# Block means turned in quarters of the TensorE array, the last result tile written in halves, and a new instruction order

## Chip, cores and metric

The kernel runs on one core of a Trainium2 chip. The metric is the device time of one execution in microseconds (us); the median of the runs shown is compared before and after.

## Reference

Sparse attention followed by a two-layer feed-forward part. q, k and v are 4 batch elements x 8 heads x 768 positions x 64. Every query attends to the keys less than 16 positions away, and to 24 block keys, each the maximum over 32 positions; the block values are the means over the same 32 positions.

```
k_sum = k.reshape(B, H, nb, 32, D).max(axis=3)
v_sum = v.reshape(B, H, nb, 32, D).mean(axis=3)
scores_l = where(|i - j| < 16, scale * q @ k.T, -1e9)
scores_s = scale * q @ k_sum.T + log(32)
a = softmax(concat(scores_l, scores_s))
x = a @ concat(v, v_sum)             # then to 3072 tokens x 512
h = x @ w_in                         # 512 x 2048
out = (h - tanh(h)) @ w_out          # 2048 x 512
```

## The kernel before

**Units of work.** The 3072 tokens are cut into 8 units u of 384 tokens, two for each batch element b = u // 2. Attention goes by head pairs p (4 in a unit), each as a chain: turn q and k on TensorE ("turn"), scores into PSUM banks pS0 and pS1, minimum, exponential, sum and normalisation, turning the probabilities ("p turn"), and the product with the values into bank pX ("values"). The 24 block keys and block values lie beside the window's keys and values in the tiles k and vw. The feed-forward part goes by 16 blocks f of the hidden size: products into bank pH ("in"), tanh and its relatives on ScalarE, one product on GpSimd or VectorE ("g"), a split into a high and a low part (gh, gl), and products into the three result banks pY0 to pY2 ("out"). From u = 2 on, units are taken in pairs and the first products come from sums of weights that lie in DRAM (scr) and are loaded into wraw.

**Block means.** For b = 0 and 1, `place_v` makes the mean of four heads (a group g) with 24 matmuls whose four outputs lie at PSUM partitions 0, 32, 64 and 96, each a quarter of the array's columns, and copies them head by head into the tile `mean`, on ScalarE or VectorE. For b = 2 and 3, `sum_chunks` adds the 32 positions of each block on GpSimd (vacc) and takes their maximum on VectorE (kacc). Then `finish_k` turns kacc in bank pS1 and copies it to th, and `finish_v` brings vacc into `mean`: four matmuls with slices of the identity (the "mean turn"), all into partitions 0 to 23 of pS1 at columns 64 x head, and one ScalarE copy of 24x256 with the factor 1/32 ("mean out"). That happens four times in the kernel: two groups for b = 2, two for b = 3. `put_mean` then sends `mean` to vw by DMA from SyncE ("mean put", vw<-mean).

**Results.** `store_y` copies each result tile of 128x512 from its pY bank by ScalarE and stores it by one DMA of 256 KB ("y out", "y store"). The last unit's three tiles end the kernel. After that the program reads one number, the largest sum of squares that it saw ("seen"), and leaves out a second, exact version of itself if it is small.

**Order.** No engine's order is written by hand. Each operation is given to `Plan.add` with an assumed cost on each engine that may do it, its reads and its writes. `Plan.schedule` then lists all operations once: at each step the engine that comes free first takes the ready operation with the highest level. A level is the longest path of assumed costs to the end, plus a number from the table BIAS for that single operation and a number from KB for its kind and phase. SL holds, by kind, phase and engine, how much sooner a second engine must be for it to get the operation. The order of all engines, SyncE's DMA queue among them, and the choice of engine thus come from these tables. The instructions of nearly all operations are recorded under line 76, the one that passes them on, so the profile is read by tiles.

Of the kernel before, what the change touches and what calls it, by code (L numbers as in the profile page):

```python
# [47 lines left out]
SIGNED = set()

SL = {('g', 0, 'vector'): 2, ('g', 1, 'vector'): 0, ('g', 2, 'vector'): -0.3, ('g high', 0, 'vector'): 2.5, ('g high', 1, 'vector'): -0.6, ('g high', 2, 'vector'): 0.3, ('g low', 0, 'vector'): 4, ('g low', 1, 'vector'): -0.6, ('g low', 2, 'vector'): 0, ('k first', 0, 'vector'): 0.3, ('k first', 1, 'vector'): 1.5, ('k first', 2, 'vector'): -0.6, ('k high', 0, 'vector'): 4, ('k high', 1, 'vector'): 2, ('k high', 2, 'vector'): -0.3, ('k keep', 0, 'vector'): 2.5, ('k keep', 1, 'vector'): 2, ('k keep', 2, 'vector'): 1, ('k move', 0, 'vector'): -0.6, ('k move', 0, 'gpsimd'): 1, ('k move', 1, 'vector'): -0.3, ('k move', 1, 'gpsimd'): 4, ('k move', 2, 'vector'): 4, ('k move', 2, 'gpsimd'): 2, ('mean out', 0, 'vector'): 0.6, ('mean out', 1, 'vector'): 4, ('mean out', 2, 'vector'): 2, ('normal', 0, 'scalar'): 2, ('normal', 0, 'gpsimd'): 2.5, ('normal', 1, 'scalar'): 0.6, ('normal', 1, 'gpsimd'): -0.3, ('normal', 2, 'scalar'): 0, ('normal', 2, 'gpsimd'): 0, ('p out', 0, 'vector'): 4, ('p out', 1, 'vector'): 4, ('p out', 2, 'vector'): 0, ('part', 0, 'vector'): 0.3, ('part', 1, 'vector'): 0, ('part', 2, 'vector'): 0.6, ('q high', 0, 'vector'): 1.5, ('q high', 1, 'vector'): 1, ('q high', 2, 'vector'): 0.6, ('s high', 0, 'vector'): -0.3, ('s high', 1, 'vector'): 4, ('s high', 2, 'vector'): -0.3, ('s low', 0, 'gpsimd'): 2, ('s low', 1, 'gpsimd'): 2, ('s low', 2, 'gpsimd'): 0.6, ('s mix', 0, 'gpsimd'): -0.6, ('s mix', 1, 'gpsimd'): 0.3, ('s mix', 2, 'gpsimd'): 4, ('s whole', 0, 'gpsimd'): 1.5, ('s whole', 1, 'gpsimd'): 1, ('s whole', 2, 'gpsimd'): 0, ('sum guard', 0, 'gpsimd'): 0.3, ('sum guard', 1, 'gpsimd'): 1.5, ('sum guard', 2, 'gpsimd'): -0.3, ('top high', 0, 'scalar'): -0.6, ('top high', 1, 'scalar'): -0.3, ('top put', 0, 'vector'): 0, ('top put', 0, 'scalar'): 1, ('top put', 1, 'vector'): 2.5, ('top put', 1, 'scalar'): 0.6, ('top put', 2, 'vector'): 2.5, ('top put', 2, 'scalar'): 0.3, ('w high part 2', 0, 'vector'): 0.3, ('w high part 2', 1, 'vector'): 2.5, ('w high part 2', 2, 'vector'): 2.5, ('w scale', 0, 'vector'): -0.6, ('w scale', 1, 'vector'): 0.3, ('w scale', 2, 'vector'): 0, ('x high', 0, 'vector'): 0.6, ('x high', 1, 'vector'): 4, ('x high', 2, 'vector'): 2.5, ('x low', 0, 'gpsimd'): -0.3, ('x low', 1, 'gpsimd'): 0, ('x low', 2, 'gpsimd'): 2, ('x mix', 0, 'gpsimd'): 0.3, ('x mix', 1, 'gpsimd'): 0, ('x mix', 2, 'gpsimd'): 1.5, ('x whole', 0, 'vector'): 0.6, ('x whole', 1, 'vector'): -0.3, ('x whole', 2, 'vector'): 2}  # L50

KB = {('chunk load', 0): 434.7, ('chunk max', 0): 88.2, ('chunk max', 1): -2.7, ('chunk sum', 0): -220.5, ('chunk sum', 1): -359.7, ('const', 0): -85, ('const', 1): -136.2, ('const', 2): -292.2, ('exp', 0): -33.6, ('g', 0): 13.2, ('g high', 0): -241.1, ('g low', 0): -310.4, ('in first', 0): -71.1, ('in first', 1): -182.2, ('inverse', 0): 28.8, ('join', 0): -293.9, ('join', 1): -75.7, ('k first', 0): -518.8, ('k first', 1): 106.5, ('k first', 2): 448.9, ('k high', 0): -153.3, ('k high', 1): -35.8, ('k keep', 0): 101, ('k keep', 1): -596.6, ('k keep', 2): -249.5, ('k load', 1): -310.2, ('k load', 2): -1.6, ('k move', 0): 111.7, ('k move', 1): -80.4, ('k move', 2): -200.1, ('key turn', 0): -255.8, ('key turn', 1): 120.7, ('key turn', 2): -1.5, ('mean out', 0): -253.8, ('mean out', 1): -79.7, ('mean put', 0): 93.1, ('mean put', 1): -73.6, ('mean put', 2): -2.8, ('mean turn', 1): 1.3, ('mean turn', 2): 20.1, ('min', 0): -0.6, ('normal', 0): 1.9, ('out first', 0): -357.5, ('out first', 1): -259.5, ('p out', 0): -27.4, ('p turn', 0): -1, ('part', 0): 89.2, ('part', 1): 385.1, ('q high', 0): -508.8, ('q load', 0): -35.5, ('q load', 1): 1.5, ('s high', 0): -41.2, ('s high', 1): 1.8, ('s high', 2): -462.5, ('s load', 0): -243.6, ('s load', 1): 1.6, ('s low', 0): 24.9, ('s low', 2): 102.6, ('s mix', 0): -358.8, ('s mix', 2): -480, ('s store', 0): -187, ('s store', 1): 0.7, ('s store', 2): -123.9, ('s whole', 0): 102.7, ('s whole', 1): -1.9, ('s whole', 2): 130.5, ('scores', 0): 1.4, ('seen', 0): 90.1, ('seen', 1): -77, ('seen', 2): -428.9, ('seen max', 0): -210.6, ('seen max', 1): 358.7, ('seen max', 2): 451.2, ('seen turn', 0): -0.7, ('seen turn', 1): 422.3, ('seen turn', 2): -9.1, ('series', 0): -201.9, ('square', 0): -65.5, ('sum', 0): 2.4, ('sum', 1): 419.6, ('sum', 2): -916.3, ('sum guard', 0): 59.1, ('tanh', 0): -2.1, ('top high', 0): 522.9, ('top high', 1): -162.7, ('top max', 0): 10.2, ('top max', 1): 238.5, ('top max', 2): -133.8, ('top pre', 0): -43.1, ('top pre', 1): 183.6, ('top pre', 2): -330.8, ('top put', 0): 0.1, ('top put', 1): -866.6, ('top put', 2): -26.1, ('top turn', 1): -172.1, ('top turn', 2): -472.6, ('turn', 0): 50.1, ('turn', 1): 211.7, ('v load', 1): -28.3, ('values', 1): -139.4, ('w high part 2', 0): -476.2, ('w high part 2', 1): 18.5, ('w high part 2', 2): -45.7, ('w load', 2): 227.6, ('w low', 2): 254.3, ('w low part 2', 0): -652.5, ('w low part 2', 1): -319, ('w low part 2', 2): -478.7, ('w scale', 2): -271.5, ('w shift', 1): 10.3, ('w shift', 2): -314.7, ('w sign', 0): -86.7, ('w sign', 2): -126.7, ('x high', 0): 646, ('x high', 1): -12, ('x low', 0): 282.9, ('x low', 2): -2, ('x mix', 0): 644.6, ('x mix', 1): 18, ('x whole', 0): -1.1, ('x whole', 1): -240.3, ('y out', 0): 157.1, ('y store', 0): -402.7}

HALF = {'const': (12, 12), 'k load': (33, 52), 'q load': (12, 24), 'top pre': (16, 16), 'v load': (44, 82), 'top turn': (8, 8), 'top max': (8, 8), 'q turn': (6, 15), 'q high': (12, 30), 'k turn': (6, 15), 'k high': (6, 15), 'top put': (7, 15), 'scores': (6, 14), 'sum': (8, 8), 'min': (30, 84), 'exp': (30, 84), 'sum out': (8, 8), 'sum guard': (5, 26), 'inverse': (5, 26), 'normal': (30, 84), 'p turn': (15, 42), 'p out': (15, 41), 'mean turn': (2, 4), 'mean out': (2, 4), 'mean put': (6, 14), 'values': (4, 4), 'x whole': (4, 9), 'w load': (13, 32), 'w scale': (12, 32), 'w shift': (12, 32), 'w low': (11, 32), 'w sign': (11, 32), 'w high part 2': (11, 32), 'w low part 2': (7, 32), 'in': (5, 33), 'square': (5, 33), 'tanh': (5, 32), 'series': (5, 32), 'g': (4, 32), 's store': (5, 48), 'out': (7, 96), 'x high': (0, 10), 'x low': (0, 10), 'y out': (0, 6), 'y store': (0, 6), 'g high': (0, 16), 'g low': (0, 16), 's whole': (0, 16), 's mix': (0, 32), 's high': (0, 16), 's low': (0, 16), 'chunk load': (0, 10), 'chunk max': (0, 4), 'chunk sum': (0, 4), 's load': (0, 3), 'x mix': (0, 1), 'top high': (0, 0), 'part': (0, 0), 'join': (0, 0), 'seen': (0, 0), 'seen turn': (0, 0), 'seen max': (0, 0), 'w high part': (3, 26), 'w low part': (3, 26), 'w sign 1': (4, 12), 'w sign 2': (4, 12), 'top low': (1, 2), 'cube': (2, 18), 'big': (2, 17), 'direct': (2, 17), 'pick': (2, 17), 'q low': (0, 2), 'q again': (0, 2), 'k low': (0, 2), 'k again': (0, 2)}


# [254 lines left out]
def program(  # L311
# [433 lines left out]
    def finish_v(b, g, tag):  # L745
        acc, ps = ("acc", 1, b, g), bank(("mv", b, g), tag)

        def go():
# [668 lines left out]
```

## Time and profile before

| what | value |
|---|---|
| median of 3 runs | 685.15 us (684.44, 685.15, 686.1) |
| the profiled execution, its own time | 684.28 us |
| its span, first to last instruction | 682.6 us |
| granted TensorE clock, mean | 0.996 |
| TensorE busy | 659.1 us, 97% |
| ScalarE, VectorE, GpSimd busy | 491.2, 417.4, 206.8 us |
| HBM traffic over the span | 172 GB/s |

PE is TensorE's matmul, PEld its weight load, DVE VectorE, ACT ScalarE, POOL GpSimd, SPq SyncE's queue, which issues the DMAs. A row of the timeline has the start, the time, the engine, the line, the operation, the tiles written and read, and in brackets the idle time before it with what ended it. A matmul's time runs until its results are out, so that rows of PE overlap; the distance between starts is what a matmul takes of the array. In a table of stages, the busy time of each engine stands with its count of instructions, then the granted clock (PEclk), the share of the DMA engines and the bytes moved.

### The profile page before, as it was taken

The page shows a single profiled execution, that of the slowest core. Times are in us where ns is not written, and L with a number is a line of the kernel's source. Part 1 is how long each engine was busy: PE and PEld are TensorE (multiplying, and loading weights), DVE is VectorE, ACT ScalarE, POOL GpSimd, SP SyncE. Part 2 cuts the span into 40 slices and gives each one's busy share as a digit, 9 for nine tenths or more (in the row PEclk, how much of TensorE's full clock was granted, in tenths as well). Part 3 has the DMA queues.
Part 4 walks back from the last instruction along what each step waited for, and adds up shares of the span by engine and source line. Part 5 has one row for each costly group of instructions (what it writes and reads, how often), then busy time and mean ns, then how long its engine had stood idle before and what let it go on. Part 6 is the DMA issues. An engine that isn't in the chain of part 4 may idle for free.

```text
span 682.6 us, 14370 instructions
## 1 busy us (share of the span) xinstructions
PE 659.1 (97%) x4885; PEld 549.1 (80%) x4885; DVE 417.4 (61%) x1183; ACT 491.2 (72%) x1445; POOL 206.8 (30%) x336
## 2 busy tenths in 40 slices
PE   7899999899999989999999999999999999999995
PEld 6665555478888877999888889899889889999884
DVE  3889988868897476555584574445576443323551
ACT  4888576778787787768984786766679946555882
POOL 2012222325355545312375642321124110000230
PEclk9999999999999998999999999999999999999999
DMA  8899999853766864785576456758435214453101
GB/s 242 218 260 286 292 291 271 275 156 136 214 190 192 269 186 135 192 220 172 133 233 187 119 139 211 221 156 213 141 116 158 105 62 147 161 170 123 48 1 52
DMA packets 145151, 121.05 MB, mean 177 GB/s; under 512 B 85036, under 2 KB 110892, under 8 KB 145068
## 3 DMA queue, kind: packets, MB, share of 16 engines
q1 hardware_dynamic: 145068, 120.03, 59.6%
q8 instruction: 41, 0.67, 0.4%
q14 instruction: 42, 0.34, 0.2%
HBM read 94.57 MB, written 23.07 MB: 172 GB/s over the span
## 4 chain that ended last, share of the span: by engine, by line
PE 85%; DMA 7%; DVE 3%; ACT 1%; SPq 1%; issue 1%; POOL 1%; ACTq 0%; POOLq 0%; DVEq 0%
PE pY L76 37%; PE pH L76 36%; PE pS L76 7%; PE pX L76 5%; DMA tmp<-in_k_dram 2%; SPq L76 1%; DMA wraw<-in_moe_w_in_dram 1%; DMA gu<-in_v_dram 1%; DMA wh<-in_k_dram 1%; DVE kacc L76 1%; DVE wraw L76 1%; DMA vw<-mean 1%; DMA rawk<-in_k_dram 1%; DMA out_dram<-tmp 1%; DMA scr<-wraw 1%
## 5 line engine op out<-in xcount | busy, mean ns | idle before, releaser
L76 PE MATMUL pY<-wf,gh 128*128 128x512 f32 x432 | 178.1, 439 | 2.9 <-POOL gh L76 2.9
L76 PE MATMUL pH<-wh,wraw 128*128 128x384 f32 x672 | 175.5, 342 | 0.1
L76 PE MATMUL pY<-wh,gh 128*128 128x512 f32 x336 | 137.0, 408 | 0.0
L76 PE MATMUL pY<-wh,gl 128*128 128x512 f32 x336 | 132.7, 395 | 0.0
L76 PEld LDWEIGHTS pH<-wh,wraw 128*128 128x128 f32 x672 | 121.4, 189 | 8.8 <-issue 1.2
L76 PE MATMUL pH<-wf,wraw 128*128 128x384 f32 x309 | 104.2, 337 | 0.0
L76 ACT ACTIVATE prob<-prob,stat 128x118 f32<-128x118 f32 x247 | 92.5, 384 | 12.7 <-DVE stat L76 11.3
L76 PEld LDWEIGHTS pY<-wf,gh 128*128 128x128 f32 x432 | 80.2, 189 | 25.4 <-issue 10.6
L76 PEld LDWEIGHTS pY<-wh,gl 128*128 128x128 f32 x336 | 63.2, 188 | 13.8
L76 POOL TENSOR_TENSOR gu<-gu,gt 128x384 f32<-128x384 f32 x31 | 33.7, 1087 | 128.8 <-ACT gu L76 127.7
L76 PEld LDWEIGHTS pY<-wh,gh 128*128 128x128 f32 x336 | 63.3, 188 | 10.9 <-issue 1.7
L76 ACT ACTIVATE gu<-gu 128x384 f32<-128x384 f32 x128 | 66.6, 521 | 1.8
L76 PE MATMUL pH<-o,wf 128*128 128x384 f32 x188 | 65.1, 442 | 2.0 <-ACT o L76 1.7
L76 PEld LDWEIGHTS pH<-wf,wraw 128*128 128x128 f32 x309 | 58.1, 188 | 0.0
L76 ACT ACTIVATE gu<-pH 128x384 f32<-128x384 f32 x65 | 31.7, 488 | 36.5 <-PE pH L76 33.5
L76 DVE CUSTOM_DVE_ANT_0 prob<-pS,mask 128x118 f32<-128x118 f32 x180 | 40.1, 275 | 28.8 <-PE pS L76 28.8
L76 PEld LDWEIGHTS pH<-o,wf 128*128 128x128 f32 x188 | 34.8, 189 | 19.7 <-issue 2.9
L76 ACT ACTIVATE gv<-pH 128x384 f32<-128x384 f32 x60 | 29.0, 484 | 27.0 <-PE pH L76 26.8
L76 DVE TENSOR_TENSOR gl<-gu,gh 128x384 fp32r<-128x384 f32 x43 | 27.0, 628 | 32.6 <-ACT gh L76 31.8
L76 POOL COPY k<-th 64x72 f32<-64x72 f32 (+1 forms) x45 | 12.7, 282 | 107.9 <-PE pS L76 86.3
L76 DVE TENSOR_TENSOR gu<-gu,gt 128x384 f32<-128x384 f32 x39 | 23.3, 596 | 35.9 <-ACT gu L76 35.8
L76 POOL TENSOR_TENSOR gl<-gu,gh 128x384 fp32r<-128x384 f32 x27 | 29.2, 1081 | 50.8 <-ACT gh L76 28.9
(211 smaller groups left out, 1242.5 us busy)
## 6 DMA issues: line engine op xcount, KB each, us to landing
wraw<-scr SPq DMA_DIRECT2D x75, 512.0 KB
wraw<-in_moe_w_in_dram SPq DMA_DIRECT2D x16, 512.0 KB
wraw<-in_moe_w_out_dram SPq DMA_DIRECT2D x16, 512.0 KB
scr<-wraw SPq DMA_DIRECT2D x16, 512.0 KB
rawq<-in_q_dram SPq DMA_DIRECT2D x42, 128.0 KB
out_dram<-tmp SPq DMA_DIRECT2D x21, 256.0 KB
wraw<-scr SPq DMA_DIRECT2D x21, 256.0 KB
scr<-wh SPq DMA_DIRECT2D x16, 256.0 KB
```

Of the source, the lines that this page charges most:

```text
L76: return lambda *args, **kwargs: self._tc.keep_in_program_order(op(*args, **kwargs))
```

## The change

1. In `finish_v` the four matmuls write at partitions 32 x head, columns 0 to 63, in place of partitions 0 to 23, columns 64 x head. The copy into `mean` is four copies of 24x64, each on ScalarE or VectorE. The assumed costs follow: 0.2 for the turn in place of 0.56, and 0.2 or 0.17 for each copy in place of one of 0.28.
2. In `store_y` the last tile of the last unit is copied in two halves of 128x256, the first by ScalarE and the second by VectorE, and stored by two DMAs of 128 KB (1024-byte rows in place of 2048).
3. The tables BIAS, SL and KB are new. Of 3304 entries of BIAS 11 stay as they are and 3349 are there after; of the 83 entries of SL 17 stay; of KB none.

```
-                tensor.matmul(at(ps)[:NB, D * hh:D * (hh + 1)], ident[:96, NB * hh:NB * (hh + 1)], at(acc)[:96], start=True, stop=True)
-        do("mean turn", PE, 0.56, go, r=[(acc, 0), IDENT], w=[(ps, 0)])
-        do("mean out", ACT, 0.28, lambda: scalar.activation(mean[32 * g:32 * g + NB], at(ps)[:NB, :HG * D], AF.Copy, scale=1.0 / 32), r=[(ps, 0)], w=MEANS[g])
+                tensor.matmul(at(ps)[32 * hh:32 * hh + NB, :D], ident[:96, NB * hh:NB * (hh + 1)], at(acc)[:96], start=True, stop=True)
+        do("mean turn", PE, 0.2, go, r=[(acc, 0), IDENT], w=[(ps, 0)])
+        for n in range(HG):
+            either("mean out", {ACT: 0.2, DVE: 0.17}, lambda e, n=n: copy(e, mean[32 * g:32 * g + NB, D * n:D * (n + 1)], at(ps)[32 * n:32 * n + NB, :D], 1.0 / 32), r=[(ps, 0)], w=[MEANS[g][n]])
...
-        do("y out", ACT, 0.48, lambda: scalar.activation(at(ys), at(y), AF.Copy, scale=1.0 / (3.0 * EA * EC) if small_only else 1.0), r=[(y, 0)], w=[(ys, 0)])
-        r = u * U + P * i
-        dma("y store", lambda: sync.dma_start(out[r:r + P, :], at(ys)), P * DM * 4, 2048, r=[(ys, 0)])
+        r, by, n = u * U + P * i, 1.0 / (3.0 * EA * EC) if small_only else 1.0, 2 if end and i == NT - 1 else 1
+        for h in range(n):
+            x = slice(DM // n * h, DM // n * (h + 1))
+            if h:
+                do("y out", DVE, 0.335, lambda x=x: vector.tensor_scalar(at(ys)[:, x], at(y)[:, x], by, None, op0=ALU.mult), r=[(y, 0)], w=[(ys, h)])
+            else:
+                do("y out", ACT, 0.48 / n, lambda x=x: scalar.activation(at(ys)[:, x], at(y)[:, x], AF.Copy, scale=by), r=[(y, 0)], w=[(ys, h)])
+            if n > 1:
+                dma("y store", lambda x=x: sync.dma_start(out[r:r + P, x], at(ys)[:, x]), P * DM * 4 // n, 1024, r=[(ys, h)])
+        if n == 1:
+            dma("y store", lambda: sync.dma_start(out[r:r + P, :], at(ys)), P * DM * 4, 2048, r=[(ys, 0)])
```

More of the change, by code (lines that the diff above doesn't have):

```diff
@@ new lines @@
+SL = {('g', 0, 'vector'): 0, ('g', 1, 'vector'): 0.3, ('g', 2, 'vector'): 0.3, ('g high', 0, 'vector'): 2, ('g high', 1, 'vector'): 0.3, ('g high', 2, 'vector'): 0.3, ('g low', 0, 'vector'): -0.6, ('g low', 1, 'vector'): 0.3, ('g low', 2, 'vector'): 0, ('k first', 0, 'vector'): 1, ('k first', 1, 'vector'): 0, ('k first', 2, 'vector'): -0.3, ('k high', 0, 'vector'): 2.5, ('k high', 1, 'vector'): 2, ('k high', 2, 'vector'): 0, ('k keep', 0, 'vector'): 2.5, ('k keep', 1, 'vector'): 1, ('k keep', 2, 'vector'): 2.5, ('k move', 0, 'vector'): 0.3, ('k move', 0, 'gpsimd'): 2, ('k move', 1, 'vector'): 0, ('k move', 1, 'gpsimd'): 1.5, ('k move', 2, 'vector'): 2.5, ('k move', 2, 'gpsimd'): 1.5, ('mean out', 0, 'vector'): 2, ('mean out', 1, 'vector'): 1.5, ('mean out', 2, 'vector'): -0.6, ('normal', 0, 'scalar'): 2, ('normal', 0, 'gpsimd'): 2.5, ('normal', 1, 'scalar'): 0.6, ('normal', 1, 'gpsimd'): -0.6, ('normal', 2, 'scalar'): -0.3, ('normal', 2, 'gpsimd'): -0.6, ('p out', 0, 'vector'): 4, ('p out', 1, 'vector'): 2, ('p out', 2, 'vector'): 0, ('part', 0, 'vector'): 0, ('part', 1, 'vector'): 1, ('part', 2, 'vector'): 0.3, ('q high', 0, 'vector'): 1.5, ('q high', 1, 'vector'): 0.3, ('q high', 2, 'vector'): 4, ('s high', 0, 'vector'): 1.5, ('s high', 1, 'vector'): 4, ('s high', 2, 'vector'): 2, ('s low', 0, 'gpsimd'): 0.3, ('s low', 1, 'gpsimd'): 1.5, ('s low', 2, 'gpsimd'): 0, ('s mix', 0, 'gpsimd'): 0.3, ('s mix', 1, 'gpsimd'): 2, ('s mix', 2, 'gpsimd'): 4, ('s whole', 0, 'gpsimd'): 2.5, ('s whole', 1, 'gpsimd'): 2, ('s whole', 2, 'gpsimd'): 0.6, ('sum guard', 0, 'gpsimd'): -0.3, ('sum guard', 1, 'gpsimd'): 1.5, ('sum guard', 2, 'gpsimd'): -0.6, ('top high', 0, 'scalar'): -0.6, ('top high', 1, 'scalar'): -0.3, ('top put', 0, 'vector'): 0.6, ('top put', 0, 'scalar'): 2.5, ('top put', 1, 'vector'): 4, ('top put', 1, 'scalar'): 4, ('top put', 2, 'vector'): 1, ('top put', 2, 'scalar'): 2, ('w high part 2', 0, 'vector'): 0.6, ('w high part 2', 1, 'vector'): 4, ('w high part 2', 2, 'vector'): 0.6, ('w scale', 0, 'vector'): 0.6, ('w scale', 1, 'vector'): -0.6, ('w scale', 2, 'vector'): -0.3, ('x high', 0, 'vector'): 1, ('x high', 1, 'vector'): 2.5, ('x high', 2, 'vector'): 1.5, ('x low', 0, 'gpsimd'): 0.3, ('x low', 1, 'gpsimd'): 0.6, ('x low', 2, 'gpsimd'): 1.5, ('x mix', 0, 'gpsimd'): 2, ('x mix', 1, 'gpsimd'): 2, ('x mix', 2, 'gpsimd'): 1.5, ('x whole', 0, 'vector'): 2, ('x whole', 1, 'vector'): -0.3, ('x whole', 2, 'vector'): 1}
@@ new lines @@
+KB = {('chunk load', 0): -89.6, ('chunk max', 0): -366.8, ('chunk max', 1): 28.1, ('chunk sum', 0): 57.1, ('chunk sum', 1): 190.1, ('const', 0): 65.2, ('const', 1): 43.2, ('const', 2): -106.1, ('exp', 0): 243.7, ('g', 0): -0.4, ('g high', 0): 224, ('g low', 0): 581.2, ('in first', 0): -297, ('in first', 1): -122.7, ('in first', 2): 3.9, ('inverse', 0): 159.2, ('join', 0): 267.6, ('join', 1): 205.6, ('k first', 0): 207.9, ('k first', 1): -179.9, ('k first', 2): 120.7, ('k high', 1): -5, ('k keep', 0): -62.1, ('k keep', 1): -284.8, ('k keep', 2): 236.2, ('k load', 0): 0.8, ('k load', 1): -360, ('k move', 0): 211.7, ('k move', 1): 31.1, ('k move', 2): -140, ('key turn', 0): -515.5, ('key turn', 1): 651.5, ('key turn', 2): -247, ('mean out', 0): -207.7, ('mean out', 1): 254.1, ('mean put', 0): 31.1, ('mean put', 1): -1.9, ('mean turn', 2): -184.3, ('min', 0): 2, ('normal', 0): -184.1, ('out first', 0): -160.8, ('out first', 1): -350.3, ('p out', 0): -85.4, ('p turn', 0): 73.1, ('part', 0): 447.8, ('part', 1): 235.8, ('q high', 0): -17.3, ('q high', 2): -171.7, ('q load', 0): 48.1, ('q load', 2): -1.1, ('s high', 0): 422.3, ('s high', 2): -195.5, ('s load', 0): 39.6, ('s low', 0): -326.9, ('s low', 2): -95.2, ('s mix', 0): -30.5, ('s mix', 2): 31.9, ('s store', 0): -226.5, ('s store', 2): 42.5, ('s whole', 0): -65.9, ('s whole', 1): -4.1, ('s whole', 2): 175.3, ('scores', 0): 63.7, ('seen', 0): 104.1, ('seen', 1): 81.7, ('seen', 2): -463.2, ('seen max', 0): 101.2, ('seen max', 1): 138.7, ('seen max', 2): -333.8, ('seen turn', 0): 12.5, ('seen turn', 1): -347, ('seen turn', 2): -55.1, ('series', 0): 69.8, ('square', 0): -2.3, ('sum', 0): -14, ('sum', 1): 22.3, ('sum', 2): 149.9, ('sum guard', 0): 88.2, ('tanh', 0): -77.3, ('top high', 0): -474, ('top high', 1): 245.5, ('top max', 0): -240.8, ('top max', 1): -368.4, ('top max', 2): -125, ('top pre', 0): -10, ('top pre', 1): 165.1, ('top pre', 2): 306.5, ('top put', 0): -149.7, ('top put', 1): -548, ('top put', 2): -247.2, ('top turn', 1): 299.5, ('top turn', 2): -288.3, ('turn', 0): -175.4, ('turn', 1): -6.8, ('v load', 0): 25.6, ('values', 0): 20.7, ('values', 1): -90.2, ('w high part 2', 0): -63.2, ('w high part 2', 1): -228.7, ('w high part 2', 2): -172.1, ('w load', 0): -70.7, ('w load', 1): -15.4, ('w load', 2): -449.1, ('w low', 0): -229.2, ('w low', 1): 8.3, ('w low', 2): 154, ('w low part 2', 0): 54.4, ('w low part 2', 1): -9, ('w low part 2', 2): -241.3, ('w scale', 0): -180.3, ('w scale', 1): 3, ('w scale', 2): 70.5, ('w shift', 0): 173.9, ('w shift', 1): 4.6, ('w shift', 2): 120.4, ('w sign', 0): 37.6, ('w sign', 2): -204.1, ('x high', 0): 80.1, ('x high', 1): -57, ('x low', 0): 329.4, ('x low', 1): -4.3, ('x mix', 0): 230.5, ('x mix', 1): -410.1, ('x whole', 0): 60.1, ('x whole', 1): -34.8, ('y out', 0): -294.9, ('y store', 0): 23.1}
```

4 lines of the change are left out of this document (1 added, 3 removed).

## Prediction

> **What bounds the kernel now.** I read the page's busy line and chain first, then a table of three stages, then two of its rows more finely, and last PE's own waits.
>
> ```profile
> span 682.6 us, 14370 instructions
> PE 659.1 (97%) x4885; PEld 549.1 (80%) x4885; DVE 417.4 (61%) x1183; ACT 491.2 (72%) x1445; POOL 206.8 (30%) x336
> PE 85%; DMA 7%; DVE 3%; ACT 1%; SPq 1%; issue 1%; POOL 1%; ACTq 0%; POOLq 0%; DVEq 0%
> ```
> ```profile
> 0.00:40.00 40.00, 31.80 (x572) 26.48 (x572) 25.02 (x112) 25.13 (x86) 6.94 (x34) 1.00 0.86 243
> 40.00:640.00 600.00, 591.59 (x4160) 493.47 (x4157) 376.35 (x1041) 439.30 (x1292) 190.51 (x294) 1.00 0.62 183
> 640.00:682.60 42.60, 35.66 (x159) 29.11 (x157) 16.04 (x32) 26.73 (x68) 9.30 (x8) 0.98 0.11 40
> ```
> ```profile
> 120.00:160.00 40.00, 37.08 (x290) 26.63 (x288) 31.73 (x92) 30.18 (x96) 14.81 (x15) 1.00 0.68 207
> 240.00:280.00 40.00, 36.61 (x308) 31.80 (x310) 24.81 (x68) 30.57 (x97) 19.25 (x38) 0.96 0.59 160
> ```
> ```profile
> PE pS L76 <- POOL ident L76: 4.3, 1, 4.3
> PE pY L76 <- POOL gh L76: 2.9, 1, 2.9
> PE pX L76 <- DMA rawk<-in_k_dram: 2.1, 1, 2.1
> ```
>
> TensorE is the bound: busy 97% of the span, 85% of the chain. Its idle time lies in three places. The start has 40.00 - 31.80 = 8.2 us, of which 4.3 is the wait for the identity that GpSimd makes first; no part of the change touches that. The 600 us between have 600 - 591.59 = 8.41 us, and two of the fifteen 40 us stages in them hold 2.92 + 3.39 = 6.31 of it. The end has 42.60 - 35.66 = 6.94 us. So work taken from PE anywhere in the middle counts almost fully, and what an order can win there is mostly those two stages. They are two accidents:
>
> ```profile
> 127.84 5.08 POOL L76 TENSOR_TENSOR gh<-gu,gt 128x384 f32<-128x384 f32 x1 [4.68 <-DVE tmp L76]
> 132.97 1.13 PE L76 MATMUL pY<-wf,gh 128*128 128x512 f32 x2 [2.92 <-POOL gh L76]
> ```
> ```profile
> 256.71 0.44 PE L76 MATMUL pX<-ident,rawk 128*128 128x128 f32 x2 [2.09 <-DMA rawk<-in_k_dram]
> ```
> ```profile
> 256.70:258.00 1.30, 1.29 (x8) 1.09 (x8) 1.30 (x3) 1.22 (x4) 1.14 (x3) 0.86 1.05 386
> 258.00:259.50 1.50, 1.50 (x6) 1.21 (x5) 1.05 (x3) 1.13 (x5) 1.34 (x3) 0.50 1.00 292
> 259.50:261.00 1.50, 1.50 (x6) 1.50 (x5) 0.00 (x0) 0.61 (x2) 1.02 (x4) 0.50 0.68 205
> 261.00:264.00 3.00, 3.00 (x17) 2.71 (x17) 1.47 (x3) 1.78 (x5) 2.60 (x6) 0.99 0.36 88
> ```
>
> At 127.84 one GpSimd product took 5.08 us, and PE waited 2.92 for it. At 256.71 PE waited 2.09 us for a load of keys, and straight after it ran for 3.00 us at a granted clock of 0.50 and for 1.30 us at 0.86: 3.00 x 0.50 + 1.30 x 0.14 = 1.7 us more, 3.8 in all. The Trainium skill ("TensorE: Matmul & The Clock Gate", Part 1) says that the clock halves only after about one idle window of 3.4 us, in windows that run free of the kernel. This trace differs: 2.09 us were enough here, and 2.92 us at 132.97 were not. By the page alone the second accident would cost 2.1 us.
>
> **The mean turn (part 1).** Before:
>
> ```profile
> 234.48 0.34 PE L76 MATMUL pH<-wf,wraw 128*128 128x384 f32 x1
> 234.75 0.63 PE L76 MATMUL pS<-vacc,ident 96*24 96x64 f32 x8
> 235.31 0.50 PE L76 MATMUL pY<-wh,gh 128*128 128x512 f32 x1
> ```
> ```profile
> L76 PE MATMUL pS<-vacc,ident x32: 216/219/237, 234.8 to 396.3; 96*24 96x64 f32 x32
> ```
> ```profile
> 93.52 0.88 PE L76 MATMUL pS<-wh,wh 128*32 128x64 f32 x48
> 94.33 0.70 PE L76 MATMUL pY<-wf,gh 128*128 128x512 f32 x1
> ```
>
> One turn (four matmuls, eight records) holds the array 235.31 - 234.75 = 0.56 us. The quarter form has a row already: `place_v`'s 48 records, also in quarters, hold it 94.33 - 93.52 = 0.81 us, so a round of eight takes 0.81 / 6 = 0.135. A lone round cannot overlap the next one. It lies between 0.135 and the 0.219 of one record; I take 0.20, nearer the latter. That saves 0.56 - 0.20 = 0.36 a turn, 4 x 0.36 = **-1.44 us**. All four lie in the middle, where PE is the bound. If a turn is followed by a wait for a load, its 0.36 only lengthens that wait, so the gain could shrink towards 0. The lower end is 4 x (0.56 - 0.135) = -1.7. The upper end is that the array must empty once more on each side of the quarter form; the nearest row for that is the gap that PE's weight queue shows before the old form:
>
> ```profile
> 234.75 0.46 PEld L76 LDWEIGHTS pS<-vacc,ident 96*24 96x24 f32 x8 [0.25 <-issue]
> ```
>
> A turn would then take 0.20 + 2 x 0.25 = 0.70 in place of 0.56, and the four +0.6. I keep -1.44, because the old form already enters through a gap and `place_v`'s 0.81 us is taken to the next product's start, its way out included. The Trainium skill ("TensorEngine Tiling (Array Packing)", Key Properties) says that changing the tiling mode drains TensorE, which speaks against the change; no run here separates that drain from the gap above, and by the page alone the turn would gain less than 1.44.
>
> **Mean out.** One copy becomes four:
>
> ```profile
> L76 ACT ACTIVATE mean<-pS 24x64 f32<-24x64 f32 x8 | 1.7, 216 | 0.1
> L76 ACT ACTIVATE mean<-pS 24x256 f32<-24x256 f32 x4 | 1.5, 371 | 0.9 <-PE pS L76 0.8
> L76 DVE COPY mean<-pY 24x64 f32<-24x64 f32 x2 | 0.4, 214 | 0.3 <-PE pY L76 0.3
> ```
> ```profile
> 267.22 0.61 PE L76 MATMUL pS<-vacc,ident 96*24 96x64 f32 x8 [0.43 <-ACT th L76]
> 267.87 0.37 ACT L76 ACTIVATE mean<-pS 24x256 f32<-24x256 f32 x1 [0.79 <-PE pS L76]
> 268.61 0.33 PE L76 MATMUL pS<-k,q 64*64 64x118 f32 x4
> ```
>
> That is 4 x 0.216 - 0.371 = 0.49 us more ACT or DVE time at each turn, 2.0 in all. ACT is idle for 28% of the span and DVE for 39%, which hides it. The cover fails only where the next scores want bank pS1 soon. That is the turn at 267.22: copy until 268.24, scores at 268.61. Afterwards the turn ends 0.36 earlier, at about 267.4; four copies on ACT alone run to about 268.4, and the scores could start at 268.61 - 0.36 = 268.25. So 0.15 us of the gain goes back there, 0 if DVE takes two copies, and 0.5 if ACT has another operation between. I take **+0.1**. SyncE's mean put waits for the four copies; after this turn it was issued at 270.16, 1.9 us after the copy, so it and the loads behind it keep their place:
>
> ```profile
> 270.16 0.81 SPq L76 DMA_DIRECT2D vw<-mean  x1
> ```
>
> **The last tile (part 2).**
>
> ```profile
> 675.27 0.39 PE L76 MATMUL pY<-wh,gl 128*128 128x512 f32 x1
> 675.70 1.08 ACT L76 ACTIVATE wraw<-pY 128x512 f32<-128x512 f32 x2 [1.46 <-PE pY L76]
> 676.32 0.82 SPq L76 DMA_DIRECT2D out_dram<-wraw  x2
> ```
> ```profile
> L76 DVE COPY probT<-pS 118x256 f32<-118x256 f32 x12 | 5.0, 422 | 6.5 <-PE pS L76 6.4
> L76 ACT ACTIVATE probT<-pS 118x256 f32<-118x256 f32 x48 | 18.0, 382 | 5.5 <-PE pS L76 5.3
> ```
>
> Two full copies follow each other on ACT, 675.70 to 676.78; two stores follow from 676.32 at 0.41 each, the second at about 676.8. Then comes the landing and the program's end at 682.6. With halves, DVE's 0.42 runs beside ACT's first copy and is done at 676.12; ACT's half ends at about 676.6. There are then three issues, at 676.15, 676.56 and 676.97: the last one 0.17 later, but with 128 KB behind it in place of 256. At an estimated 0.33 MB per us, between the 183 GB/s of the middle and the 386 of the fullest row above and nearer the latter because nothing else moves, 128 KB are about 0.4 us. I take 0.17 - 0.4 = **-0.2**. The ends are -0.6 (the second copy gone from the path and the store first in line) and +0.4 (one more issue of 0.41 and nothing gained).
>
> **The new order (part 3).** Every engine's order changes, SP's queue and POOL's with it, and no row shows the result. Its price is bounded by the accidents: 2.9 and 3.8 us, mean 3.3. Both gone gives -6.7; two more gives +6.7. If a stage goes wrong with the frequency seen, 2 in 15, a new draw of fifteen stages has none with chance 0.12, one 0.27, two 0.29, three 0.19, more 0.13. One and two are about equally likely. The middle between them is -1.65; the value that halves the whole draw is -0.4. I take **-1.0** between the two.
>
> **Sum.** -1.44 + 0.1 - 0.2 - 1.0 = -2.5 us. The profiled execution took 684.28 us by its own time, its span plus 1.7, and becomes 681.7. It lies 0.87 under the median of the runs, 685.15; against that median the forecast is **682.6 us**.
>
> **The rivals.**
> 1. *One more late load.* The place is the reload of keys and queries ahead of a "turn", as at 256.71: SP's queue holds the rawk loads behind chunk loads and mean puts, the new order sets it anew, and a PE shorter by 0.36 a turn arrives sooner. With the same two accidents and a third of 3.8 us the time is 685.15 - 1.54 + 3.8 = 687.4. It decides from a wait of 1.54 + 1.37 = 2.9 us, the lost clock included. For it: 3.8 us did occur in a stage whose DMA engines were only 0.59 busy, so it was a matter of order. Against it: in thirteen of the fifteen stages no such wait is there. Chance 0.20, more accidents included.
> 2. *The quarter form gains nothing*, because the array empties around it or because the gain falls into a following wait, and the order is as good as the old: 685.15 + 0.1 - 0.2 = 685.1. For it: the 0.25 gap, and that 256.71's wait comes after a turn; against it: `place_v`'s 0.135 a round. Chance 0.18.
> 3. *The order has no accident*: 685.15 - 1.54 - 6.7 = 676.9. For it: both waits are single rows; against it: the planner's fixed costs cannot see a GpSimd product of 5.08 us, and such a one can come back at another place. Chance 0.10.
>
> **How the numbers follow.** The forecast, one or two accidents with the direct gain, has the remaining 0.52; its own range is 685.15 - 1.54 - 3.3 = 680.3 to 683.9. About 0.2% (1.37 us) is what a measurement of this kernel can tell from no change, so faster means below 683.78. That holds 0.48 of the forecast and rival 3: 0.58. The other 0.04 of the forecast and rival 2 are the same: 0.22. Rival 1 is slower: 0.20. The range leaves out rival 3 and the worse half of rival 1: 678.6 to 687.4.
>
> **What would show it.** Right: the eight vacc records hold PE about 0.2 us; PE's busy time falls by about 1.4; the interior idle time is 8.4 or less, without a row of 5 us on GpSimd and without a stage under clock 0.97; the end after the last matmul is 6.7 or so in place of 6.94. Wrong: the vacc records still take 0.5; scores wait for `mean`; a PE wait above 2 us on rawk, vw or a GpSimd product at a new place; or a start that loses more than its 8.2 us, which I have counted as unchanged.

## The result: 1.4% slower, and the profile after

| | before | after |
|---|---|---|
| median of four runs | 685.62 us | 695.58 us (693.09, 693.58, 697.58, 698.09) |
| ratio, 95% interval | | 1.0139 [1.011, 1.0168] |
| span of the profiled execution | 682.6 us | 696.4 us (its own time 698.09) |

A run more than 1.5% above the fastest of its kernel counts as slow and stays out of the ratios; that happened once, at 703.69 us in experiment 4. The profiled execution after is the longest of its four and the one before is shorter than all of its four, so the spans lie 13.8 us apart where the medians lie 10.0.

The page after, its busy line and its chain:

```profile
span 696.4 us, 14377 instructions
PE 669.0 (96%) x4895; PEld 552.3 (79%) x4895; DVE 426.5 (61%) x1210; ACT 486.8 (70%) x1432; POOL 197.5 (28%) x335
PE 78%; DMA 9%; ACT 4%; POOL 3%; SPq 3%; DVE 2%; issue 1%; DVEq 0%; POOLq 0%; ACTq 0%
```

TensorE's share of the chain falls from 85% to 78%; DMA, ScalarE, GpSimd and SyncE's queue share what it loses. TensorE idles 27.4 us (696.4 - 669.0) in place of 23.5, and its busy time is 9.9 us longer for nearly the same instructions. About half of that is the clock. Three stretches of the table of stages after, each at a granted clock of 0.50, where before had one, priced at 1.7 us in the prediction:

```profile
31.46:38.30 6.84, 6.28 (x41) 4.51 (x41) 4.56 (x11) 2.35 (x6) 0.64 (x1) 0.50 0.75 202
140.70:144.10 3.40, 3.40 (x48) 2.47 (x44) 0.81 (x5) 0.98 (x4) 0.24 (x1) 0.50 0.16 36
260.20:263.60 3.40, 3.40 (x29) 2.71 (x30) 1.87 (x14) 2.17 (x10) 1.73 (x4) 0.50 0.93 221
```

They are 6.84 + 3.40 + 3.40 = 13.64 us at half speed, so by estimate 6.8 us lost against 1.7 before: 5.1 more. With the 3.9 of idle time that is 9.0 of the 13.8 us between the spans. The rest lies mostly in the start. The planner fills gaps of TensorE at the start with products of the identity with itself (`keep_warm`, pS<-ident), which feed no result: 11.9 us in place of 8.3, a part of them inside the half-clock stretches. And one turn in the first 11 us (pH<-ident,gt, 48 records) took 3.23 us in place of 1.79. So the true idle time grew by more than the profile's 3.9 us.

Where in the span it is lost can be read from the mean turns, which are the same work in both kernels. Timeline rows after, then the third and fourth of before (its first two, 234.75 and 267.22, are shown in the prediction):

```profile
240.62 0.31 PE L76 MATMUL pS<-vacc,ident 96*24 96x64 f32 x8
240.86 0.62 PE L76 MATMUL pH<-wh,wraw 128*128 128x384 f32 x2
273.95 0.31 PE L76 MATMUL pS<-vacc,ident 96*24 96x64 f32 x8
378.05 0.31 PE L76 MATMUL pS<-vacc,ident 96*24 96x64 f32 x8
405.76 0.31 PE L76 MATMUL pS<-vacc,ident 96*24 96x64 f32 x8 [1.11 <-POOL vacc L76]
688.68 0.39 PE L76 MATMUL pY<-wh,gl 128*128 128x512 f32 x1
```
```profile
369.34 0.63 PE L76 MATMUL pS<-vacc,ident 96*24 96x64 f32 x8
395.93 0.63 PE L76 MATMUL pS<-vacc,ident 96*24 96x64 f32 x8
```

The changed kernel is 5.9 us late at the first turn, 6.7 at the second, 8.7 at the third, 9.8 at the fourth and 13.4 at the last product (688.68 against 675.27). What TensorE waited for, from its list of waits after:

```profile
PE pH L76 <- DMA wraw<-scr: 3.1, 4, 1.8
PE pS L76 <- DVE prob L76: 3.0, 2, 2.3
PE pX L76 <- DMA vw<-in_v_dram: 2.6, 2, 2.0
PE pY L76 <- POOL gh L76: 2.6, 1, 2.6
```

Before had two waits of 2 us or more besides the identity. Now there are three (softmax 2.29, GpSimd 2.61, values 2.00), each with a half-clock stretch 0.5 to 1.4 us behind it, and a fourth of 1.81 for sums of weights.

The first of them is in the start. VectorE and TensorE of the changed kernel at 27 to 31 us, and the same 3.41 us stage of after, then of before:

```profile
29.68 0.43 DVE L76 TENSOR_SCALAR tmp<-wraw 128x512 f32<-128x512 f32 x1 [2.52 <-DMA wraw<-in_moe_w_in_dram]
30.49 1.23 DVE L76 TENSOR_SCALAR prob<-prob,stat 128x118 f32<-128x118 f32 x6
31.01 1.04 PE L76 MATMUL pS<-ident,prob 128*118 128x128 f32 x4 [2.29 <-DVE prob L76]
```
```profile
28.05:31.46 3.41, 1.11 (x22) 0.84 (x17) 1.77 (x9) 1.77 (x5) 0.00 (x0) 1.00 1.07 376
```
```profile
28.05:31.46 3.41, 1.95 (x36) 1.69 (x31) 2.99 (x11) 3.11 (x12) 0.49 (x2) 1.00 0.88 225
```

VectorE's new order puts the scaling of the first weight block ahead of six softmax normalisations that do not need it. The weights landed late, so the normalisations came at 30.49, TensorE was busy for 1.11 us of the 3.41 (1.95 before), and the clock was then 0.50 for 6.84 us.

### The profile page after: what moved, and what is told of

The parts are those of the page before. It is cut to its first block, busy times and chain, and to the rows that moved or that the text cites. A ratio compares the mean times of both kernels' runs of the same rounds, so it can differ in the third digit from the quotient of the medians.

```text
span 696.4 us, 14377 instructions
## 1 busy us (share of the span) xinstructions
PE 669.0 (96%) x4895; PEld 552.3 (79%) x4895; DVE 426.5 (61%) x1210; ACT 486.8 (70%) x1432; POOL 197.5 (28%) x335
## 4 chain that ended last, share of the span: by engine, by line
PE 78%; DMA 9%; ACT 4%; POOL 3%; SPq 3%; DVE 2%; issue 1%; DVEq 0%; POOLq 0%; ACTq 0%
PE pY L76 34%; PE pH L76 33%; PE pS L76 6%; PE pX L76 5%; DMA wraw<-scr 3%; SPq L76 3%; DMA tmp<-in_v_dram 2%; DMA tmp<-in_k_dram 1%; DMA wraw<-in_moe_w_out_dram 1%; POOL tmp L76 1%; ACT prob L76 1%; POOL gh L76 1%; DMA rawq<-in_q_dram 1%; DMA wraw<-in_moe_w_in_dram 1%; DMA vw<-in_v_dram 1%
## 5 line engine op out<-in xcount | busy, mean ns | idle before, releaser
L76 ACT ACTIVATE prob<-prob,stat 128x118 f32<-128x118 f32 x238 | 89.6, 385 | 14.7 <-DVE stat L76 14.2
L76 DVE TENSOR_TENSOR gl<-gu,gh 128x384 fp32r<-128x384 f32 x53 | 33.5, 632 | 38.2 <-ACT gh L76 35.4
L76 POOL TENSOR_TENSOR gu<-gu,gt 128x384 f32<-128x384 f32 x28 | 30.2, 1080 | 87.2 <-ACT gu L76 85.6
L76 POOL TENSOR_TENSOR prob<-prob,stat 128x118 f32<-128x118 f32 x72 | 34.3, 491 | 50.3 <-DVE stat L76 45.3
```

Source lines behind the costliest of these rows:

```text
L76: return lambda *args, **kwargs: self._tc.keep_in_program_order(op(*args, **kwargs))
```

## Experiments

In all of them the order of every engine is a fixed list, taken from the planner of one kernel or edited; lines that stand at 76 then stand at 83 or 85. Each ratio is to the kernel before, run on the same chip in the same series, and its brackets are a 95% interval.

```
-    for t in plan.schedule((0.214, keep_warm)):
+    for t in forced():        # the list ORDER
```

**1. Forms and order apart.** Two kernels: both new forms in the order of before, and the new order with the old turn, one copy and a whole last tile.

```
forms_old_order:       ORDER = before, QUARTER = True,  HALVES = True
new_order_old_forms:   ORDER = after,  QUARTER = False, HALVES = False
```

> The order of before, operation for operation, with the two new forms put in at the old places: the mean turn in quarters with four ScalarE copies in a row, the last tile in halves. Theory A (the loss is the new order's, the forms gain): about 1.5 us faster than before, near 684; eight vacc records in about 0.2 us. Theory B (the forms themselves lose, by an array that empties around the quarter form and by a longer end): 687 or more, vacc records still about 0.5 us, the end after the last result copy longer by about 1 us.

> The order of the changed kernel with the old forms put back: the mean turn into one partition range with one copy, the last tile whole. Theory A: no better than the changed kernel, 694 to 698. Theory B: back near before, under 688.

Measured: 686.73 us, ratio 1.0006 [0.998, 1.0033], and 695.53 us, ratio 1.0136 [1.0057, 1.0214]. The loss is the order's: with the old forms the new order is as slow as the changed kernel. The forms together show no gain and no loss in the old order, which lies between the two theories for the first run; the second run came as its theory A.

**2. Quarter form alone in the old order.**

```
QUARTER = True, HALVES = False     # ORDER = before
```

> The order of the kernel before with the quarter form of the mean turn alone; the last tile is whole, one copy and one store. Theory A (a turn is 0.316 us shorter and the gain reaches the end; what cancelled it when both forms were put in the old order were the halves, whose third store issue took 2.45 us): 1.3 us faster than before, ratio 0.998. Theory B (the gain falls into waits for loads and block sums right behind the turns, the halves cost nothing): ratio 0.9995 to 1.0005.

Measured: 684.97 us, ratio 0.9971 [0.9949, 0.9993], about 2 us faster [0.5, 3.5]. The quarter form gains about what it saves in the array: theory A. What took the gain away in experiment 1 then came with the halves, as far as two intervals that just overlap can tell. The tail of the profile of experiment 1: its last three stores as a group, ScalarE's last copies and VectorE's half:

```profile
L83 SPq DMA_DIRECT2D out_dram<-wraw x3: 332/377/2452, 675.8 to 676.7; - x3
```
```profile
675.19 0.87 ACT L83 ACTIVATE wraw<-pY 128x512 f32<-128x512 f32 x2 [1.46 <-PE pY L83]
676.09 0.42 DVE L83 TENSOR_SCALAR wraw<-pY 128x256 f32<-128x256 f32 x1 [4.06 <-ACT wraw L83]
```

One store's issue, the last one, held SyncE for 2.45 us where the others take 0.33 to 0.38. The three kernels below with the old tail and halves show 2.01, 2.07 (experiment 3) and 0.91 (experiment 8) there; with the tail of the new order none is above 0.37.

**3. Cuts: where in the order the loss lies.** One order up to a planned time, then what is left in the other order; both new forms.

```
new_start_old_rest:  after's list up to 136 (first unit), then before's
old_start_new_rest:  before's up to 136, then after's
new_to_u1_old_rest:  after's up to the second unit's end, then before's
old_to_u1_new_rest:  before's up to the second unit's end, then after's
old_to_u3_new_rest:  before's up to the fourth unit's end, then after's
```

> New forms. The order of the changed kernel for all that it places in its first 136 planned us (unit 0), then the order of before for the rest. If the start carries the loss seen up to unit 0's last result copy (146.0 us before, 153.7 after): 7 to 8 us over the forms in the old order, about 691. If the loss is spread over the late waits: about 685.

> New forms. The order of before for its first 136 planned us, then the order of the changed kernel. If the start carries 7 to 8 us: about 688. If the loss is made by the late waits on loads (weights sums, values) alone: about 694.

> Both new forms; the new order up to the planned end of the second unit, the order of before from there. Theory A (the new start and the first two units lose 4 to 6 us, the rest of the loss lies behind): 690 to 692.5 us. Theory B (all of the loss lies here): 693.5 to 696.5.

> Both new forms; the order of before up to the planned time at which the second unit ends (about 235 us of the run), the new order from there, so that the seam lies outside the first unit. Theory A (the stages between 240 and 420 us lose 4 to 6 us): 690 to 693 us, waits for loads and softmax between 250 and 425 us. Theory B (they lose nothing by themselves, the loss lies ahead of 240 us): 685.5 to 688, as the run with the new order only from unit 3's end.

> Both new forms; the order of before up to the planned time at which unit 3 ends (about 407 us of the run), the new order from there. Theory A (the new order loses nearly all of its time in the start and in the attention of the third and fourth batch element between 240 and 420 us): as both forms in the old order, 685 to 687.5. Theory B (it loses throughout, behind 420 us as well, through loads of weight sums that come late): 689 to 692.

| kernel | median us | ratio, interval |
|---|---|---|
| new_start_old_rest | 690.25 | 1.0053 [1.0015, 1.0091] |
| old_start_new_rest | 696.72 | 1.013 [1.0072, 1.0188] |
| new_to_u1_old_rest | 688.87 | 1.0071 [1.0028, 1.0113] |
| old_to_u1_new_rest | 695.65 | 1.0144 [1.0097, 1.0192] |
| old_to_u3_new_rest | 687.0 | 1.0006 [0.9979, 1.0033] |

The last row equals the forms in the old order, so behind the fourth unit the new order loses little. It may lose some 2 us there: the forms in the old order end with the long store issue of experiment 2, and this kernel, with the new tail, does not. The first two units cost 0.7% (the first alone 0.5%), and the third and fourth, 240 to 420 us, about 1.4%. The sum, 2.1%, is more than the 1.4% of the whole; the intervals allow about 0.4 and 1.0. Also, the kernels that end in the old order have the long issue in their share, and a seam between two orders may cost something itself (in old_start_new_rest the seam lies inside the first unit, whose last result copy came at 153.18, 7 us late, though its start was the old one). So both stretches lose, by these medians the later one more; the exact shares stay open. Of the five expectations, the first and the last came as one of their theories said; the other three medians lay outside both of theirs.

The longest waits of TensorE between 240 and 420 us, first with the new order in that stretch (old_to_u1_new_rest), then with the old one (old_to_u3_new_rest):

```profile
PE pS L83 <- POOL vacc L83: 2.3, 1, 2.3
PE pS L83 <- ACT prob L83: 2.2, 2, 1.5
PE pX L83 <- DMA vw<-in_v_dram: 1.5, 1, 1.5
PE pS L83 <- DVE prob L83: 1.1, 1, 1.1
```
```profile
PE pH L83 <- DMA wraw<-scr: 1.8, 1, 1.8
PE pX L83 <- DMA rawk<-in_k_dram: 1.5, 1, 1.5
PE pX L83 <- DMA vw<-mean: 1.4, 2, 1.0
PE pS L83 <- POOL vacc L83: 1.2, 1, 1.2
```

With the new order TensorE waits for softmax (2.2 + 1.1 = 3.3 us), values and block sums. With the old one softmax is nearly in time (0.7 us in that profile), and the waits are mostly for loads and block sums. The first of these profiles is of the shortest of its four runs (690.84; the others 693.96 to 697.68) and the second of one of the longest of its ten (690.52), so the lists show the kind and not the size.

**4. The start mended.** Seven operations ahead of one on VectorE:

```
-  w scale 0, inverse 2, w shift 0, normal 15, 14, 16, 12, 17, 13
+  inverse 2, normal 15, 14, 16, 12, 17, 13, w scale 0, w shift 0
```

> The changed kernel with its own order, but on VectorE the softmax operations of the third pair (one reciprocal and six normalisations) stand ahead of the first weight block's scaling, which waits for a late weight load. Theory A (that wait at 27 to 30 us starves TensorE and halves its clock at 31.5 to 38.3): the wait of 2.29 us at 31.01 and the half-clock stretch go, first unit's last result 3.5 to 5.7 us earlier than 153.7, so 690 to 692 us in place of 695.6. Theory B (the start lags because the whole beginning is arranged otherwise, the wait is only where it shows): the wait comes back at the next step, 694.5 to 696.5.

Measured: 693.18 us, the median of three runs (689.76 to 694.76; the fourth is the one of 703.69), ratio 1.0108 [1.0049, 1.0166]; the interval overlaps the changed kernel's. The profile, VectorE and TensorE at the mended place, and the clock of the first 40 us:

```profile
26.88 1.24 DVE L83 TENSOR_SCALAR prob<-prob,stat 128x118 f32<-128x118 f32 x6
28.10 0.66 PE L83 MATMUL pS<-ident,prob 128*118 128x128 f32 x4
31.49 0.71 PE L83 MATMUL pS<-ident 128*128 128x128 f32 x4 [1.85 <-ACT probT L83]
124.42 0.60 PE L83 MATMUL pX<-ident,rawk 128*128 128x128 f32 x4
147.62 0.60 PE L83 MATMUL pX<-ident,rawk 128*128 128x128 f32 x4
```
```profile
0.00:40.00 40.00, 34.46 (x601) 28.66 (x601) 23.97 (x111) 25.77 (x87) 7.76 (x36) 1.00 0.82 229
```

The same two key turns before and after, then the first of them and the first 40 us in the kernel of experiment 6, whose start is that of the changed kernel:

```profile
122.89 0.60 PE L76 MATMUL pX<-ident,rawk 128*128 128x128 f32 x4
147.34 0.60 PE L76 MATMUL pX<-ident,rawk 128*128 128x128 f32 x4
```
```profile
125.73 0.60 PE L76 MATMUL pX<-ident,rawk 128*128 128x128 f32 x4
153.31 0.60 PE L76 MATMUL pX<-ident,rawk 128*128 128x128 f32 x4
```
```profile
124.37 0.60 PE L83 MATMUL pX<-ident,rawk 128*128 128x128 f32 x4
```
```profile
0.00:40.00 40.00, 32.65 (x598) 26.80 (x599) 22.75 (x107) 25.35 (x85) 7.78 (x36) 1.00 0.80 226
```

The normalisations come 3.6 us sooner, and TensorE then waits 1.85 us at the next step: theory B, mostly. At the first key turn (124.42) the mended kernel is 1.3 us ahead of the changed one. But the kernel of experiment 6, whose clock stayed at 1.00 there in its profiled execution (last row), reaches it at 124.37 without the edit. So the edit adds nothing measurable.

Nor is that lead all due to the half clock. The turn that ends the wait starts at 31.01 in the changed kernel and at 30.08 in that of experiment 6, so 0.93 of the 1.4 us were lost before the clock fell. The one place ahead of it where the changed kernel is clearly slower lies in the first 11 us: the turn named above took 3.23 us in place of 1.79, its matmuls 332 ns in place of 229. (The clock column reads 1.00 in that stretch, but these traces hold no clock record before 10.98 and 4.74 us.) The half-clock stretch itself then costs about 0.5 us net here, and neither loss falls in every execution.

The 4.4 us more by which the mended kernel leads at the second key turn (5.7 - 1.3) are another matter: its product on GpSimd at 133 took 2.08 us in place of 4.94, so the wait of 2.61 us and the 1.7 us lost at half clock behind it are not there.

**5. GpSimd's product.** The product that took 4.94 us at 134.35 goes to VectorE; then a kernel with the start of experiment 4 and two such products on VectorE.

```
-  g 14  gpsimd
+  g 14  vector           # second kernel: g 4 and g 14, and the start mended
```

> The changed kernel with its own order, but the feed-forward product that took 4.94 us on GpSimd at 134.35 is done by VectorE. Theory A (it is that one product on GpSimd beside VectorE's back-to-back instructions): TensorE's wait of 2.61 us at 139.3 and the half clock at 140.7 to 144.1 go, 691 to 693 us. Theory B (the operands of that stage are late anyway, or VectorE, now busier, becomes late): 694.5 to 697.

> The new order with the softmax ahead of the weight scaling at the start, and with the two products that took up to 9.97 us (at 64) and 4.94 us (at 134) on GpSimd done by VectorE. Theory A (those products are what spreads the runs of the new order, and the start is worth 5 us): 688.5 to 691.5, the runs within 2 us of each other, no row above 2.5 us on GpSimd for gh. Theory B (VectorE has no room for them): 693 or more.

Measured: 697.42 us (694.65 to 704.14), ratio 1.0169 [1.0131, 1.0208], and 694.73 us (693.16 to 698.47), ratio 1.0102 [1.0073, 1.0132]. The profile of the first is of its longest run (704.14). In it the wait at 139 is gone, but another product had become longer. GpSimd's products as a group (shortest, median, longest in ns), TensorE's wait for it, and the engines' busy time while it ran:

```profile
L83 POOL TENSOR_TENSOR gh<-gu,gt x11: 990/1044/9970, 49.6 to 153.0; 128x384 f32<-128x384 f32 x11
```
```profile
74.11 6.06 PE L83 MATMUL pY<-wf,gh 128*128 128x512 f32 x8 [8.46 <-POOL gh L83]
```
```profile
64.09:74.06 9.97, 1.57 (x4) 0.38 (x2) 9.12 (x19) 3.93 (x8) 9.97 (x2) 0.73 1.05 309
```

The same product of 128x384 takes 1.04 us as a rule and 9.97 here, while VectorE ran 19 instructions with hardly a gap (9.12 of 9.97 us). It ended less than a microsecond after VectorE's run did. The Trainium skill ("SBUF — State Buffer", Who interferes with whom) says that a VectorE instruction with two SBUF inputs contends with a GpSimd instruction that reads SBUF. The trace agrees: 16 of the 19 were tensor_tensor or scalar_tensor_tensor. Here GpSimd was slowed over a whole row of instructions; that the two inputs are the reason was not tried by itself. In the second kernel no such product is above 2.2 us, yet the median is still 694.73 and the runs spread over 5 us. So theory A's time and spread are wrong, and the long products are not the bulk of the loss. At 121.48 TensorE waits 1.34 us for a product on VectorE in that kernel, as theory B has it.

**6. Six loads sooner.** In SyncE's queue, in the new order with its own start:

```
v load 86 before q load 22; v load 115 before q load 30; q load 33 before chunk load 29
s load 36, 61, 62 each right behind what they depend on
```

> The changed kernel with its own order, but six loads moved ahead in SyncE's queue: three window loads (values for 259 and 347 us, queries for 398) and three loads of weight sums (for 424 and 512 us). Theory A (from the first unit's end to the last the new order loses 5 to 6 us because loads stand too far back in SyncE's queue): the waits of 2.00, 0.63, 1.03, 1.81 and 0.86 us and the half clock at 260.2 to 263.6 mostly go, last tile of unit 0 to last of unit 7 takes 528 to 531 us in place of 535.4, total 689 to 692. Theory B (the queue as a whole is too full, moving one load delays another): waits on loads come back at other places, 694 to 697.

Measured: 695.58 us, ratio 1.0159 [1.0112, 1.0205], unchanged. The five waits named are gone, and others stand near them:

```profile
268.15 0.68 PE L83 MATMUL pS<-ident,prob 128*118 128x128 f32 x2 [1.91 <-ACT prob L83]
397.89 0.63 PE L83 MATMUL pX<-ident,rawk 128*128 128x128 f32 x4 [1.39 <-DMA rawk<-in_k_dram]
```

With the values in time TensorE arrives earlier at the softmax and waits there, the half clock comes back right there (267.56 to 270.98), and keys take the place of queries. Theory B.

**7. All three edits together.**

> All three edits on the new order together: softmax ahead of the weight scaling at the start, six loads sooner in SyncE's queue, one product on VectorE. Theory A (these few places are the whole loss): the gains add up, 682 to 687 us, that is the kernel before or better. Theory B (the order is worse throughout, or other waits step in): 689 us or more.

Measured: 693.91 us (692.86 to 696.13), ratio 1.0127 [1.0094, 1.0159]. These few places are not the loss, then: theory B.

**8. The queue exchanged.** The computing engines in one order, SyncE's 549 transfers in the other.

> The changed kernel with the new order of the four computing engines, but SyncE's queue of 549 transfers in the order of before (only six stand elsewhere, where an operation needs them sooner). Theory A (the loss is the order of SyncE's queue: loads that stand too far back): 686 to 689 us. Theory B (the loss is the order of the computing engines): 692 to 697. If both orders only fit each other: above 697.

> Both new forms with the computing engines in the order of before, but SyncE's queue in the new order (all but 15 of 549 in sequence). Theory A (the queue loses): 692 to 696 us. Theory B (the computing engines lose): 685.5 to 688. If both orders only fit each other: above 690 in this run and above 697 in the other.

Measured: 744.24 us, ratio 1.0863 [1.0816, 1.0909], and 760.99 us, ratio 1.1108 [1.107, 1.1145]. Waits of the one, then of the other:

```profile
PE pH L85 <- DMA wraw<-scr: 13.9, 6, 6.3
PE pX L85 <- DMA vw<-in_v_dram: 5.8, 3, 2.9
```
```profile
PE pH L85 <- DMA wraw<-scr: 9.9, 4, 4.2
PE pS L85 <- ACT prob L85: 7.9, 5, 3.9
```

Neither theory A nor B but the third possibility: the two lists only fit each other, and a mismatch costs 59 to 76 us, several times the change's loss. About 26 and 28 us of that are the clock, by an estimate from its means of 0.962 and 0.960 over spans of 745.5 and 759.6 us, against 0.996 over 682.6. So this exchange cannot say whether the queue or the computing engines lose the 9 us.

**9. A version that beats both.** Old order, quarter form, whole last tile, GpSimd's product at 127.8 on VectorE, three loads of keys ahead of two chunk loads.

```
-  g 14 gpsimd;  k load 34, q load 20, chunk load 12, k load 35, 37, chunk load 13, k load 36
+  g 14 vector;  k load 34, q load 20, k load 35, 37, 36, chunk load 12, 13
```

> As the run with the quarter form alone in the old order, and two places mended: the product of 5.08 us on GpSimd at 127.8 is done by VectorE, and three loads of keys stand ahead of two chunk loads in SyncE's queue, so that the keys for 256.7 us land about 1 us sooner. Theory A (the two accidents cost their waits): 1.3 + 2.9 + 1 to 2.5 us faster than before, 678.5 to 680.5. Theory B (when one wait goes, the next one takes its place): 682.5 to 685.

```profile
255.61 0.43 PE L83 MATMUL pS<-ident,prob 128*118 128x128 f32 x2 [2.96 <-ACT prob L83]
```

Measured: 682.9 us (681.16 to 684.64), ratio 0.9933 [0.9909, 0.9957], by which it is 4.6 us faster than before. As a time that is theory B's; as a gain in its own series it is just short of theory A's 5.2 to 6.4 us. The waits for GpSimd at 133 and for keys at 256.7 are gone; at 255.61 TensorE waits 2.96 us for softmax instead, and the half clock follows that (256.96 to 260.37), so the keys' gain was turned into another wait.

## Why the prediction was wrong

- **The mean turn (-1.44): right.** A turn holds the array 240.86 - 240.62 = 0.24 us against 0.56, so 0.32 less and 1.3 in all; 0.20 was a little too low. No extra emptying of the array is seen: the upper end, 0.70, can be dropped. In experiment 2, where the product ahead is the same one as before, the turn starts 0.27 us behind that product's start (235.70 to 235.97), as it did before (234.48 to 234.75). The run of the form alone agrees (2 us [0.5, 3.5]). On the Trainium skill's rule that a change of tiling mode drains TensorE ("TensorEngine Tiling (Array Packing)", Key Properties): a drain of more than what lies in the 0.24 is not seen at this turn.
- **Mean out (+0.1): not contradicted.** No wait for `mean` is in the changed kernel's list for TensorE. The 0.1 is too small to be seen in a run.
- **The last tile (-0.2): wrong in sign, small here.** The step that failed is "DVE's 0.42 runs beside ACT's first copy". In experiment 1 VectorE's half begins at 676.09, when ScalarE's has just ended (675.19 + 0.87 = 676.06), and the profile puts its wait of 4.06 us down to ScalarE's copy. In the changed kernel it begins at 689.62, also behind ScalarE's end (689.49), but there VectorE was busy with "seen" until 689.50, so that row shows less. Whether the program's own dependencies or the chip keep the halves apart was not tried.

  The end after the last matmul's end is 7.2 us in the changed kernel (6.9 with its order and the whole tile), so +0.2; in the old order it is 9.3 against 7.1, +2.2, by the issue of 2.45 us. Half the bytes behind the last store gained nothing that shows. Why one issue takes 2 us more is open.
- **The new order (-1.0): this step failed.** It measured about +9 us (experiment 1). The prediction took the order as a new draw from the accidents of the old one, two stages in fifteen at 3.3 us, and wrote "Its price is bounded by the accidents". The kind of loss was right: in the profiled execution four waits (2.29, 2.61, 2.00 and 1.81) and 6.8 us at half clock make 15.5 us, against 2.92 + 2.09 + 1.7 = 6.7 before, so 8.8 more. The number of them was wrong, and the bound had no ground: experiment 8 shows lists that cost 59 to 76 us. Nor was the draw used as worked out: it gave three or more accidents 0.32, and the rival that holds them got 0.20. Why the old list has so few is not shown; that its tables had been fitted to the true times of loads and engines, and that other tables do not inherit the fit, is my reading. And the waits are no fixed set: taking them away one by one gained nothing clear of noise (experiments 4 to 7).
- **The start, "which I have counted as unchanged": wrong.** The change made every engine's list anew, so the start was in it. Even the wait for the identity, which "no part of the change touches", changed: GpSimd now makes the identity first, TensorE waits 1.41 us for it in place of 4.33, and filler products take up the time. The changed kernel is 125.73 - 122.89 = 2.8 us late at the first key turn; 1.4 of it by the slow first turn and the half clock together (experiment 4), the rest is open.
- **Rival 1 (a late load, 687.4)** had the right sign and kind, but not the place or the number. One wait of 1.03 us for queries, at 398.12, is at the place it named; the others are for values, sums of weights, softmax and block sums, at several places together.
- **The accident on GpSimd** came back, as rival 3's text held against it: 4.94 us at 134.35, beside 5.08 at 127.84 before.

Open: which property of the new list makes 240 to 420 us late. Shown is that the new order loses the time, there and in the first two units, that moving these loads, this softmax and these products by hand only moves the waits, and that queue and engines have to be judged together.

## What to carry to other kernels

When a change reorders all engines, don't price the new order by the waits that the old one has left: these were 6.7 us here, and two lists that did not fit cost 59 and 76. Split such a change, form by form in a frozen order, before judging it; here that gives a gain of 0.3% from the quarter form that the new order hid. A wait that is taken away on one engine is worth its time only if the next input is already there: the six loads gained nothing, and the keys in experiment 9 little.

## What the runs showed of the hardware

- **The clock** changes on a fixed grid within an execution. In the changed kernel it falls at 31.46, 140.69 and 260.15 us; these lie 109.23 and 119.46 us apart, which is 32 and 35 times 3.413, and each half-clock stretch lasts 3.41 or 6.83 us. What counts is how busy TensorE was in the grid's stretch just ahead. For the first fall that is 1.11 us of 3.41 (shown above); for the other two:

```profile
137.27:140.69 3.42, 1.35 (x12) 0.59 (x14) 1.16 (x2) 0.98 (x3) 2.02 (x1) 1.00 0.55 189
256.74:260.15 3.41, 1.41 (x31) 0.95 (x29) 1.49 (x5) 0.00 (x0) 0.00 (x0) 1.00 0.84 202
```

  Before, the clock fell at 257.63, after a stretch busy for 1.32 us. Going back from there by 37 times 3.413, the wait of 2.92 us that ended at 132.97 lies across two stretches, busy for 2.12 us (127.93 to 131.34) and, in the row below, 1.79:

```profile
131.34:134.76 3.42, 1.79 (x5) 1.05 (x6) 3.25 (x5) 1.47 (x4) 1.58 (x1) 1.00 0.82 274
```

  So the same wait costs its own time or 1.7 us more, by where it falls on the grid, and the grid lies elsewhere in each execution. In all eighteen profiles, the stretches at full clock that were busy for less than 0.40 of their time were each followed by half clock, those above 0.56 never, and between these either happened. The Trainium skill ("TensorE: Matmul & The Clock Gate", Part 1) speaks of at least one idle window of about 3.4 us. The length agrees; here a stretch that was idle for about 60% was enough.
- **A GpSimd product** of the same shape took 0.99 to 9.97 us. The eleven that took over 4 us (4.47 to 9.97, in eleven kernels) ran while VectorE was busy for 81 to 100% of the time, with 7 to 19 instructions.
- **A store's issue** on SyncE took 0.33 us as a rule, and 2.45, 2.07, 2.01 and 0.91 us as the last one of four kernels.
